# New due times and new groups for a list-scheduled kernel whose TensorE is nearly full

## The chip, the cores and the metric

One core of one Trainium2 chip. The time is device microseconds from the first to the last instruction, as the median of several executions. Nearly all executions of one kernel here lie within 1.5 us of its median, which is 0.3%; the worst is 2.4 us off. The kernel before took 531.44 us (530.61 to 532.65, three runs) when the prediction was made. A "look" below is one profiled execution of a kernel.

Ratios below are the mean time of one kernel's fast runs over the mean time of the other's in the same rounds on the same chip. They are not quite the ratio of the medians that are quoted beside them. The three sets of experiments ran on three chips, so ratios compare across sets and medians only roughly.

## The reference, cut to what matters

```python
# gated linear recurrence over 4 x 5824 tokens, 256 channels
a_t  = exp(8 * sigmoid(r) * log(a_base))
norm = sqrt(max(1 - a_t * a_t, 1e-6))
h    = a_t[:, t] * h + (norm * sigmoid(i) * x)[:, t]     # y[:, t] = h
# then a multiplicative feed-forward over the same 23296 tokens
out  = ((y @ w1) * (y @ w2)) @ w3 @ w_out                # 256 -> 1024 -> 1024 -> 256
```

The kernel multiplies `w3 @ w_out` once (the "fold", pieces `fold_t`, `fold_c`, `fold_m`, `fold_e`, eight of each), so that each token costs two up-projections and one down-projection. No run of this study does less.

## The kernel before: the parts that matter

The tokens are cut into 46 chunks. For each chunk, ScalarE computes tanh, decay and root, VectorE computes the gate, the scan and the product, GpSimd squares, multiplies and sometimes casts. TensorE takes the cast `y_t` through four pairs of up-projections and four down-projections:

```python
    def up(c, mp, nm, w_sb):
        pp = psum.tile([P, 2, CT], F32, name=nm, tag="pab")          # a ring of 3 for pa and pb
        for _ in range(warm.get((nm, c, mp), 0)):                      # warm-up matmuls
            nc.tensor.matmul(out=pp[:, 0, :P], lhsT=ident, rhs=ident, start=True, stop=True)
        ...                                                            # 4 matmuls of 512 columns

    def copy(c, mp):       # sa <- pa, PSUM to SBUF, on ScalarE (on VectorE if in DV_COPY): frees pa's buffer of the ring
    def product(c, mp):    # g_t <- sa * pb, on VectorE: frees pb's buffer of the ring
    def scan(c, cb):       # two of them for each chunk on VectorE, cut at a batch boundary
    def cast(c):           # y_t <- h_t, on VectorE or GpSimd
```

The ring explains most waits below. Where pairs follow each other, a `pa` takes the buffer of an earlier pair's `pb`, which the product frees. If that product stands behind a scan or a cast on VectorE, TensorE waits, although neither has anything to do with it.

The order of instructions isn't written down. A list scheduler runs inside the program that emits them: every job has a due time (a formula plus `OFFSET` by kind plus `SHIFT` by kind and chunk), each engine takes the ready job that is due first, and the result, sorted by start, is the order in which each engine's instructions are emitted. In that model, jobs of VectorE and GpSimd that carry a `lock` never overlap; its variable is called `port_free`, and "the port" below is this part of the model. What the chip does is told from the traces further down. Jobs whose `kind` needs another ScalarE table are batched by `group_sizes`; a table load took 1.28 us in the kernel before, each of its 31.

Of the kernel before, what the change touches and what calls it, by code (L numbers as in the profile page):

```python
# [20 lines left out]
def kernel(  # L21
# [28 lines left out]
    NCH = len(sizes)  # L50
    starts = [sum(sizes[:c]) for c in range(NCH)]

    group_sizes = [2, 1, 2, 3, 2, 2, 5, 4, 5, 2, 4, 4, 2, 2, 3, 3]
    assert sum(group_sizes) == NCH
    groups = []
    f = 0
    for n in group_sizes:
# [24 lines left out]
    T = {}  # L82

    N_LOG = 0
    TURN_R = {0, 1, 2, 3, 4, 5, 6, 8, 13}
    TURN_U = {0, 1, 2, 3, 5, 8, 9}
    DV_TIMES = {0, 1, 2, 8}
    DV_SQUARE = {2, 3, 10, 13}
    DV_CAST = {0, 2, 3, 7, 10, 11}
    DV_EVAC = set()  # L90
    DV_COPY = set()
    NHELD = 6
    NWF = 2
    FOLD_DMA = False
    FOLD_C, FOLD_E = "DVE", "DVE"
    W_CAST = {"w1": "POOL", "w2": "POOL", "wo": "POOL", "w3": "POOL"}
    BACKLOG = 1.05
    DUE_W, DUE_WH, DUE_W3, DUE_F = -45.0, 6.0, -22.0, 11.0
    LAG = 22.0
    D_LOAD, D_TANH, D_EXP, D_SQRT, D_GATE, D_SCAN, D_CAST = 66.0, -21.0, 2.0, 0.0, 11.5, 5.0, -14.0  # L100
    SPREAD = 4.4
    SLOT = 10.4
    M_OCC, M_LAT, M_PE = 0.04037856721, 0.02565538832, 0.0
    WARM = 80.0
    OFFSET = {"r": 8.5, "i": 8.0, "x": 6.0, "tanh_i": 3.5, "times": 3.0, "plus": -9.0, "turn_r": -12.0,
              "turn_u": -10.5, "decay": -1.5, "square": -2.0, "root": 6.5, "gated": 3.5, "scan": 0.5,
              "cast": -20.0, "copy": -1.0, "down": -3.5, "evac": -5.0, "store": -6.0}
    SHIFT = {("load", "w1"): -0.5, ("load", "w2"): 9.0, ("load", "wo"): 2.0, ("w1", 0): -27.0,
             ("w1", 1): -54.5, ("w2", 0): 2.5, ("w2", 1): -5.0, ("wo", 0): -1.0, ("wo", 1): -35.5,
             ("w3", 0): -64.5, ("w3", 1): 35.0, ("w3", 2): 4.5, ("w3", 3): 3.5, ("w3", 4): 13.0,  # L110
             ("w3", 5): 11.0, ("w3", 6): 23.5, ("w3", 7): 47.0, ("fold_t", 0): 9.5, ("fold_t", 1): -5.5,
             ("fold_t", 2): 4.0, ("fold_t", 3): 12.0, ("fold_t", 4): 2.0, ("fold_t", 5): 4.0,
             ("fold_t", 6): 1.5, ("fold_t", 7): -5.0, ("fold_c", 0): -5.5, ("fold_c", 2): 7.5,
             ("fold_c", 4): 2.5, ("fold_c", 5): 6.0, ("fold_c", 7): 11.5, ("fold_m", 0): -2.5,
             ("fold_m", 1): 2.5, ("fold_m", 2): -2.5, ("fold_m", 4): -5.5, ("fold_m", 5): 1.0,
             ("fold_m", 6): 9.5, ("fold_e", 0): 3.5, ("fold_e", 1): 2.0, ("fold_e", 2): 3.5,
             ("fold_e", 3): -4.0, ("fold_e", 4): 2.0, ("fold_e", 5): -4.5, ("fold_e", 6): 2.0,
             ("fold_e", 7): 2.0, ("r", 0): -16.0, ("r", 1): -13.0, ("r", 2): -5.5, ("r", 3): 3.5,
             ("r", 4): 3.0, ("r", 5): -6.0, ("r", 6): -0.5, ("r", 7): -6.5, ("r", 8): 0.5, ("i", 0): 1.0,
             ("i", 2): -2.0, ("i", 3): 2.0, ("i", 4): 4.0, ("i", 6): 3.5, ("i", 7): 4.0, ("i", 8): -1.5,  # L120
             ("x", 0): -2.5, ("x", 1): 1.0, ("x", 2): -1.0, ("x", 3): 1.5, ("x", 4): 5.0, ("x", 6): -4.0,
             ("x", 7): 4.5, ("tanh_r", 1): -2.5, ("tanh_r", 3): -2.0, ("tanh_r", 4): -0.5,
             ("tanh_r", 5): -1.0, ("tanh_r", 6): 2.0, ("tanh_r", 8): -3.5, ("tanh_i", 2): 4.0,
             ("tanh_i", 3): 8.0, ("tanh_i", 5): -7.5, ("tanh_i", 7): 9.0, ("tanh_i", 8): 2.0,
             ("times", 0): 3.5, ("times", 1): 2.0, ("times", 2): 5.0, ("times", 3): -8.5, ("times", 4): 5.0,
             ("times", 5): -2.0, ("times", 6): 1.0, ("times", 7): -1.0, ("times", 8): 6.0, ("plus", 0): -1.0,
             ("plus", 1): -4.0, ("plus", 2): 0.5, ("plus", 3): -1.5, ("plus", 4): 0.5, ("plus", 5): 19.5,
             ("plus", 6): 3.5, ("plus", 7): 1.5, ("plus", 8): -8.5, ("turn_r", 2): -1.0, ("turn_r", 3): 1.0,
             ("turn_r", 4): -1.0, ("turn_r", 5): -1.5, ("turn_r", 6): -4.0, ("turn_r", 8): 3.0,
             ("turn_u", 0): 1.5, ("turn_u", 1): -8.5, ("turn_u", 2): -18.0, ("turn_u", 4): 3.5,  # L130
             ("turn_u", 5): 9.5, ("turn_u", 6): -2.5, ("turn_u", 7): 3.5, ("turn_u", 8): 18.5,
             ("decay", 0): 2.5, ("decay", 1): 1.0, ("decay", 2): 5.5, ("decay", 3): -1.0, ("decay", 4): 3.0,
             ("decay", 5): 4.0, ("decay", 7): -2.5, ("decay", 8): -4.5, ("square", 1): -3.5,
             ("square", 2): 7.0, ("square", 3): -1.5, ("square", 4): 4.5, ("square", 5): -0.5,
             ("square", 6): -0.5, ("square", 8): -6.5, ("root", 0): 1.0, ("root", 1): 10.0, ("root", 2): 1.0,
             ("root", 5): -1.0, ("root", 6): -10.0, ("root", 7): 1.0, ("root", 8): 16.5, ("gated", 1): -4.5,
             ("gated", 2): -1.5, ("gated", 3): 5.0, ("gated", 5): -2.0, ("gated", 6): -3.5,
             ("gated", 7): -4.0, ("gated", 8): 1.0, ("scan", 0): 1.0, ("scan", 1): -11.5, ("scan", 2): 9.5,
             ("scan", 3): -2.0, ("scan", 4): -14.5, ("scan", 5): -6.5, ("scan", 6): 1.0, ("scan", 7): -1.0,
             ("cast", 0): 4.0, ("cast", 1): 2.0, ("cast", 3): 2.0, ("cast", 4): 1.0, ("cast", 5): -4.0,  # L140
             ("cast", 6): -1.5, ("cast", 7): -19.0, ("cast", 8): -4.0, ("pa", 1): 5.5, ("pa", 2): 23.0,
             ("pa", 3): 3.5, ("pa", 4): 2.0, ("pa", 5): -2.0, ("pa", 7): 1.0, ("pa", 8): 1.0,
             ("pb", 1): 12.5, ("pb", 2): -13.0, ("pb", 4): -0.5, ("pb", 5): 2.5, ("pb", 6): 2.5,
             ("pb", 7): -1.0, ("pb", 8): -2.0, ("copy", 0): 0.5, ("copy", 1): -1.0, ("copy", 2): 3.5,
             ("copy", 5): -2.0, ("copy", 6): -7.0, ("copy", 7): -2.0, ("product", 0): 4.5,
             ("product", 2): 2.5, ("product", 3): -2.5, ("product", 4): 0.5, ("product", 5): 2.0,
             ("product", 6): -5.0, ("product", 7): -2.5, ("product", 8): -2.0, ("down", 1): 4.5,
             ("down", 2): 3.0, ("down", 3): -2.5, ("down", 4): 12.5, ("down", 5): -1.0, ("down", 6): 3.0,
             ("down", 7): 4.0, ("down", 8): 0.5, ("evac", 2): 1.0, ("evac", 3): 1.0, ("evac", 4): 4.5,
             ("evac", 7): -6.0, ("store", 0): 8.5, ("store", 3): -3.0, ("store", 4): 3.0, ("store", 5): -4.0,  # L150
             ("store", 8): -2.0}
    src = {"r": rf, "i": jf, "x": xf}

    def flat(t):
# [7 lines left out]
    def long_rows(c):  # L162
        return c in TURN_R and c in TURN_U

# [14 lines left out]
    def tanh_r(c):  # L179
        n = sizes[c] // P  # L180
        t = gates.tile([P, NCB, 4, P], BF16, name="th_r", tag="th_r")
        if c in TURN_R:
            nc.scalar.activation(out=flat(t)[:, :n, :], in_=T["r", c][:, :n, :], func=AF.Tanh, scale=0.5)  # L183
# [129 lines left out]
    def copy(c, mp):  # L313
        w = sizes[c]
        sa = ffn.tile([P, 2, CT], BF16, name="sa", tag="sa")
        copy_to((c, mp) in DV_COPY, sa[:, :, :w], T["pa", c, mp][:, :, :w])
        T["sa", c, mp] = sa
# [20 lines left out]
    def evac(c, j2):  # L338
        T["ot", c, j2] = ffn.tile([P, 2, D], F32, name="ot", tag="ot")
        copy_to(c in DV_EVAC, T["ot", c, j2], T["po", c, j2])  # L340

# [131 lines left out]
    for k, g in enumerate(groups):  # L473
        log = k < N_LOG
        for c in g:
# [18 lines left out]
            for nm, key, tag, src_nm in (("turn_r", "pr", "rt", "thr"), ("turn_u", "pu", "ut", "u")):  # L494
                pre = ("tanh_r", c) if nm == "turn_r" else ("times", c, 1)
                d = V - D_TANH + 3.0 if nm == "turn_r" else U - D_GATE - 2.5
                if c in (TURN_R if nm == "turn_r" else TURN_U):
                    job((nm, c), "PE", 0.445 * f * (2 if c < 2 else 1), 0.445 * f * (2 if c < 2 else 1) + 0.22, d,
                        partial(turn_pe, c, key, src_nm),
                        [pre, ("ident",)] + [("turn_r", d) for d in g if nm == "turn_u" and d in TURN_R],  # L500
                        ("po", (key, c)), [(src_nm, c)])
# [37 lines left out]
            for j in range(sizes[c] // P):  # L539
# [11 lines left out]
                elif j % 2:  # L551
                    e, o, l = ("DVE", 0.599, 0.734) if c in DV_EVAC else ("ACT", 0.48, 0.63)
                    job(("evac", c, j // 2), e, o, l, t + 1.5, partial(evac, c, j // 2), [("down", c, j)],
# [18 lines left out]
    order = []  # L572
# [21 lines left out]
    while any(waiting.values()):  # L594
# [3 lines left out]
        for e in engines:  # L598
            if free[e] > t:
                continue  # L600
            key = next((k for k in waiting[e][:80] if startable(k, t)), None)
# [33 lines left out]

    nc.scalar.dma_start(out=la4, in_=a_param.rearrange("(cb p) -> p cb", p=P))

    table = None
    for _, _, key in sorted(order):
        kind = jobs[key]["kind"]  # L640
        if kind == 2 and table != 2:
            nc.scalar.preload_act_table_set("natural_log_exp_and_others")
        if kind is not None:
            table = kind
        jobs[key]["fn"]()
# [28 lines left out]
```

## Time and profile before

| what | value | read from |
|---|---|---|
| span of the profiled execution | 529.5 us | page |
| VectorE, ScalarE, GpSimd busy | 84, 87, 66% | page |

How TensorE's time divides into work and losses is worked out in the prediction below. I count TensorE's losses from start to start: the next matmul's start, less this one's start and its slot (0.056, 0.108 or 0.216 us for 128, 256 or 512 columns, after the spacing of starts at full clock: 0.056, 0.109 and 0.216 in the kernel before). Some matmul records are missing from most traces (3148 of 3204 are there in the first look at the changed kernel). One missing record of 512 columns looks like a loss of 0.216 and is left out; a real gap beside a missing record is too large by that much.

### The profile page before, as it was taken

To read this page: it belongs to the slowest core of one execution; us is meant where nothing else is said; L and a number is where in the kernel's file an instruction comes from. 1 tells how busy PE (TensorE), PEld (TensorE's weight loads), DVE (VectorE), ACT (ScalarE), POOL (GpSimd) and SP (SyncE) were. 2 spreads that over 40 slices of the span, in tenths; PEclk is the share of its full clock that TensorE was granted. 3 is DMA by queue.
4 is the path that set the end of the run, shared out by engine and by line. 5 is a ranking of instruction groups with operands and counts; after the bars stand their busy time and mean duration, and the time that the engine had idled before them with its cause. 6 is when DMAs were issued, how large, how long until landed. Compare 5 with 4: busy or idle time off the path is not lost.

```text
span 529.5 us, 8816 instructions
## 1 busy us (share of the span) xinstructions
PE 501.8 (95%) x3209; PEld 309.0 (58%) x3209; DVE 444.6 (84%) x373; ACT 459.2 (87%) x538; POOL 347.2 (66%) x270
## 2 busy tenths in 40 slices
PE   1299899999999999999999999999999999999997
PEld 1276576565655555666655565565666565665655
DVE  0798889998999988889797888898899799889642
ACT  6998698999899999989999999899999899884543
POOL 1579765569758883783878748968867677792000
PEclk9999899999999999999999999999999999999999
DMA  8999959889996998699898997969989898634112
GB/s 305 385 377 353 337 116 288 264 246 279 306 276 185 287 270 219 180 282 233 228 226 263 260 263 196 274 209 291 315 174 282 173 246 205 133 99 81 41 60 100
DMA packets 174604, 123.28 MB, mean 233 GB/s; under 512 B 84448, under 2 KB 170208, under 8 KB 174560
## 3 DMA queue, kind: packets, MB, share of 16 engines
q1 hardware_dynamic: 174288, 122.71, 85.0%
q8 instruction: 25, 0.41, 0.3%
q14 instruction: 19, 0.16, 0.1%
q10 hardware_dynamic: 272, 0.00, 0.0%
HBM read 78.91 MB, written 23.86 MB: 194 GB/s over the span
## 4 chain that ended last, share of the span: by engine, by line
PE 84%; ACT 6%; DVE 5%; issue 3%; DMA 2%; SPq 0%; DVEq 0%; ACTq 0%
PE pa L303 27%; PE pb L303 27%; PE po L334 27%; DVE g_t L323 3%; ACT sa L311 1%; PE pw L399 1%; DVE h_t L284 1%; DMA rt<-th_r 1%; ACT th_i L192 1%; ACT a_t L242 1%; DMA i_t<-in_i_gate_dram 1%; PE ptr L221 1%; ACT nrm L258 1%; DVE w3t L394 1%; ACT L192 0%
## 5 line engine op out<-in xcount | busy, mean ns | idle before, releaser
L323 DVE TENSOR_TENSOR g_t<-sa,pb 128x1024 bf16<-128x1024 bf16 (+1 forms) x184 | 219.1, 1198 | 55.5 <-ACT sa L311 47.3
L303 PEld LDWEIGHTS <-w_sb 128*128 128x128 bf16 x1472 | 144.1, 98 | 139.0 <-issue 5.0
L311 ACT CAST sa<-pa 128x1024 bf16<-128x1024 f32 (+1 forms) x184 | 183.5, 1000 | 37.5 <-PE pa L303 35.8
L303 PE MATMUL pa<-y_t,w_sb 128*128 128x512 bf16 (+1 forms) x736 | 188.3, 379 | 1.6 <-DVE g_t L323 1.3
L303 PE MATMUL pb<-y_t,w_sb 128*128 128x512 bf16 (+1 forms) x736 | 187.3, 377 | 0.6 <-DVE g_t L323 0.6
L334 PE MATMUL po<-wp_sb,g_t 128*128 128x256 bf16 x1456 | 184.5, 273 | 0.0
L334 PEld LDWEIGHTS <-g_t 128*128 128x128 bf16 x1456 | 142.4, 98 | 49.5
L284 DVE TENSOR_TENSOR_SCAN h_t<-a_t,h_t,nrm 128x512 f32<-128x512 f32 (+3 forms) x90 | 140.5, 1569 | 0.8
L249 POOL TENSOR_TENSOR nrm<-a_t 128x512 f32<-128x512 f32 (+1 forms) x84 | 107.9, 1300 | 20.9 <-ACT a_t L242 20.8
L213 POOL TENSOR_TENSOR u_t<-th_i,x_t 128x512 bf16<-128x512 f32 x78 | 116.2, 1508 | 0.5
L292 POOL CAST y_t<-h_t 128x1024 bf16<-128x1024 f32 x40 | 46.9, 1173 | 86.5 <-DVE h_t L284 72.9
L197 POOL TENSOR_SCALAR th_i<-th_i 128x1024 f32<-128x1024 f32 x42 | 53.2, 1268 | 20.6 <-ACT th_i L192 15.3
L311 ACT COPY ot<-po 128x512 f32<-128x512 f32 (+1 forms) x91 | 52.6, 580 | 15.8 <-PE po L334 14.6
L242 ACT ACTIVATE a_t<-rt,la 128x512 f32<-128x512 bf16 x74 | 58.8, 816 | 7.0 <-DMA rt<-th_r 6.1
L269 DVE SCALAR_TENSOR_TENSOR nrm<-nrm,ut 128x1024 f32<-128x1024 f32 x39 | 56.0, 1435 | 1.6 <-DMA ut<-u_t 1.6
L192 ACT ACTIVATE th_i<-i_t 128x1024 f32<-128x1024 f32 (+1 forms) x46 | 48.5, 1054 | 0.5 <-DMA i_t<-in_i_gate_dram 0.3
L258 ACT ACTIVATE nrm<-nrm 128x1024 f32<-128x1024 f32 (+1 forms) x46 | 47.6, 1053 | 0.2
L185 ACT ACTIVATE th_r<-r_t 128x1024 bf16<-128x1024 f32 x37 | 39.0, 1061 | 0.1
L221 PE MATMUL ptr<-ident,th_r 128*128 128x128 bf16 x68 | 6.8, 256 | 14.0 <-ACT th_r L183 14.0
L258 ACT ACT_TABLE_LOAD x14 | 18.0, 1283 | 0.2
L242 ACT ACTIVATE a_t<-ptr,la 128x512 f32<-128x512 bf16 (+1 forms) x18 | 12.6, 751 | 2.0 <-PE ptr L221 1.4
L221 PEld LDWEIGHTS <-th_r 128*128 128x128 bf16 x68 | 5.3, 115 | 15.3 <-ACT th_r L183 14.8
(39 smaller groups left out, 145.9 us busy)
## 6 DMA issues: line engine op xcount, KB each, us to landing
r_t<-in_r_gate_dram SPq DMA_DIRECT2D x45, 512.0 KB, 6.3
i_t<-in_i_gate_dram SPq DMA_DIRECT2D x45, 512.0 KB, 5.6
x_t<-in_x_dram SPq DMA_DIRECT2D x45, 512.0 KB, 4.9
out_dram<-ot SPq DMA_DIRECT2D x89, 256.0 KB, 3.6
wf<-in_moe_w_dram SPq DMA_DIRECT2D x12, 512.0 KB, 5.7
wf<-in_moe_w_out_dram SPq DMA_DIRECT2D x2, 512.0 KB, 6.4
ut<-u_t SPq DMA_TRANSPOSE x39, 4.5
rt<-th_r SPq DMA_TRANSPOSE x37, 4.7
```

Of the source, the lines that this page charges most:

```text
L192: nc.scalar.activation(out=t[:, :n, :], in_=T["i", c][:, :n, :], func=AF.Tanh, scale=0.5)
L197: nc.gpsimd.tensor_scalar(t, t, 1.0, 1.0, op0=ALU.add, op1=ALU.mult)
L213: nc.gpsimd.tensor_mul(out=u.rearrange("p cb j q -> p j cb q")[:, js], in0=cut(t)[:, js], in1=cut(T["x", c])[:, js])
L242: nc.scalar.activation(out=a, in_=pr, func=AF.Exp, scale=la4[:, cb:cb + 1], bias=la4[:, cb:cb + 1])
L249: eng.tensor_mul(out=T["n", c][:, cb, :w], in0=T["a", c][:, cb, :w], in1=T["a", c][:, cb, :w])
L258: nc.scalar.activation(out=T["n", c][:, :, :w], in_=T["n", c][:, :, :w], func=AF.Sqrt, scale=-1.0, bias=1.0)
L269: nc.vector.scalar_tensor_tensor(out=T["n", c][:, :, :w], in0=T["n", c][:, :, :w], scalar=1e-3, in1=T["pu", c][:, :, :w], op0=ALU.max, op1 ...
L284: nc.vector.tensor_tensor_scan(T["h", c][:, cb, lo:hi], T["a", c][:, cb, lo:hi], T["n", c][:, cb, lo:hi], init, ALU.mult, ALU.add)
L303: nc.tensor.matmul(out=pp[:, q, :w], lhsT=w_sb[:, cb, m * P:(m + 1) * P], rhs=T["y", c][:, cb, :w], start=(cb == 0), stop=(cb == NCB - 1))
L311: nc.scalar.copy(out=dst, in_=src_ps)
L323: nc.vector.tensor_mul(out=T["g", c][:, 2 * mp:2 * mp + 2, :w], in0=T["sa", c, mp][:, :, :w], in1=T["pb", c, mp][:, :, :w])
L334: nc.tensor.matmul(out=po, lhsT=T["g", c][:, k, j * P:(j + 1) * P], rhs=wp_sb[:, k, :], start=(k == 0), stop=(k == KD - 1), skip_group_che ...
```

## The change

It means to find a better order: due times, offsets, shifts and group sizes come from a longer search, in which the scheduler's model was replayed with the port taken in turns. The diff alters constants; a long one, cut to its core:

```diff
-    group_sizes = [2, 1, 2, 3, 2, 2, 5, 4, 5, 2, 4, 4, 2, 2, 3, 3]
+    group_sizes = [2, 1, 2, 3, 2, 2, 5, 4, 5, 3, 4, 2, 4, 2, 2, 3]
-    TURN_R = {0, 1, 2, 3, 4, 5, 6, 8, 13}
+    TURN_R = {0, 1, 2, 3, 4, 5, 7, 8, 13}
-    DV_EVAC = set()
-    DV_COPY = set()
+    DV_EVAC = {9}
+    DV_COPY = {(0, 1)}
-    DUE_W, DUE_WH, DUE_W3, DUE_F = -45.0, 6.0, -22.0, 11.0
+    DUE_W, DUE_WH, DUE_W3, DUE_F = -43.5, 8.0, -18.5, 12.0
-    D_LOAD, D_TANH, D_EXP, D_SQRT, D_GATE, D_SCAN, D_CAST = 66.0, -21.0, 2.0, 0.0, 11.5, 5.0, -14.0
+    D_LOAD, D_TANH, D_EXP, D_SQRT, D_GATE, D_SCAN, D_CAST = 73.5, -20.0, 4.0, -1.5, 24.0, 7.5, 19.0
...   (LAG, SPREAD, SLOT, M_OCC, M_LAT, all of OFFSET and SHIFT)
+    MOVES = []
+    plan = [key for _, _, key in sorted(order)]
+    places = {p for p, _ in MOVES}
+    rest = [key for p, key in enumerate(plan) if p not in places]
+    for p, to in MOVES:
+        rest.insert(to, plan[p])
-    for _, _, key in sorted(order):
+    for key in rest:
```

> **What bounds the kernel now.** I read the page first (shares of the span, slices), then the chain of waits, then TensorE's timeline with what ended its idle time, then windows around its gaps.
>
> ```profile
> PE 501.8 (95%) x3209; PEld 309.0 (58%) x3209; DVE 444.6 (84%) x373; ACT 459.2 (87%) x538; POOL 347.2 (66%) x270
> ...
> PE   1299899999999999999999999999999999999997
> ...
> PE 84%; ACT 6%; DVE 5%; issue 3%; DMA 2%; SPq 0%; DVEq 0%; ACTq 0%
> ```
>
> TensorE is full from the third slice on, and the chain that ended last is TensorE for 84% of the span. Its busy share counts pipelined spans, so I count issue slots instead, from start to next start. The chain shows 0.86 to 0.87 us for four 512-column matmuls (pa, pb), 0.87 for eight 256-column ones (po, pw), 0.45 for eight 128-column ones (ptr, ptw). The work is then: 360 pa/pb groups x 0.865 = 311.4, eight half-width ones x 0.435 = 3.5, 182 po groups x 0.868 = 158.0, 8 pw x 0.87 = 7.0, 8 ptw x 0.45 = 3.6, 15 ptr x 0.45 = 6.8, and 33 warm-up matmuls x 0.056 = 1.8: 492 us of a span of 529.5. So 37.5 us are lost. Where:
>
> ```profile
> 0.00:26.50 26.50, 6.11 (x48) 4.83 (x49) 11.27 (x16) 21.30 (x25) 10.28 (x14) 1.00 0.95 345
> ...
> 60.00:65.00 5.00, 4.66 (x36) 3.18 (x34) 3.82 (x4) 2.65 (x4) 4.68 (x4) 0.66 1.10 348
> ...
> 150.00:160.00 10.00, 8.66 (x53) 4.95 (x51) 9.93 (x9) 9.25 (x11) 2.54 (x2) 1.00 1.00 302
> 160.00:410.00 250.00, 250.00 (x1542) 150.67 (x1541) 221.44 (x175) 237.05 (x278) 187.36 (x142) 1.00 0.94 244
> ...
> 420.00:519.00 99.00, 99.00 (x607) 59.20 (x606) 79.28 (x63) 71.50 (x83) 48.58 (x36) 1.00 0.53 124
> ```
>
> The columns are the stretch, then busy time (and count) of TensorE, its weight load, VectorE, ScalarE, GpSimd, then clock, DMA share and GB/s. Before 26.5 us only 48 small transposes run (48 x 0.056 = 2.7 us): 23.8 us lost to filling the pipe. From 160 to 410 and from 420 to 519 TensorE has no gap at all. The rest is in few places:
>
> ```profile
> 26.50 1.80 PE L299 MATMUL pa<-ident 128*128 128x128 bf16 x15
> 28.10 1.06 PE L303 MATMUL pa<-y_t,w_sb 128*128 128x256 bf16 x4
> ...
> 36.83 1.02 PE L303 MATMUL pa<-y_t,w_sb 128*128 128x512 bf16 x4 [0.49 <-DVE g_t L323]
> ...
> 59.35 0.61 PE L385 MATMUL ptw<-ident,w_t 128*128 128x128 bf16 x8 [1.54 <-DVE wp_sb L416]
> ...
> 158.97 1.02 PE L303 MATMUL pa<-y_t,w_sb 128*128 128x512 bf16 x4 [0.81 <-DVE g_t L323]
> ...
> 519.19 7.15 PE L334 MATMUL po<-wp_sb,g_t 128*128 128x256 bf16 x64
> ```
>
> By starts: about 0.8 us lost near 36; 1.7 + 0.5 at 57 to 60; about 1.7 to the clock in 60 to 65 (5.0 us at 0.66: 5.0 x 0.34); about 1.0 at 99 to 107; about 1.8 at 153 to 159; 0.4 in scattered places. Together 8 us after the pipe is full. Another 1.9 us go to half clock between 26.5 and 30.3 (the 15 warm-up matmuls stand 0.107 us apart, not 0.056), and the tail after the last matmul's start at 526.1 is 3.4. Every wait names VectorE, most of them the product g_t that frees the PSUM pair which the next up-projection needs.
>
> [...] the busy sum of 501.8 includes overlaps, the slots sum to 492. [...] the stall at 57 to 60 is followed by a clock of 0.66 in 60 to 65. [...] a 128x512 scan takes 1.28 us when alone, 1.58 on the mean of 84, and the one at 99.58 took 2.35 as GpSimd multiplied. [...]
>
> **The change part by part.** It alters only the constants of a list scheduler that fixes the order of instructions on each engine; the launch runs the same arithmetic. MOVES is empty, so the new reordering code does nothing.
>
> - Counts. Transposes on TensorE stay 15 groups (chunk 7 in place of 6), transposes by DMA 76, table loads 31 (16 groups of chunks before and after, so no 2 x 1.28 us are saved), all matmuls but five warm-ups: 5 x 0.107 at half clock = 0.5 us. Total work of TensorE: 491.8 instead of 492.1.
> - Moved work: one 128x512 copy (chunk 0) and two 128x512 evictions of chunk 9 go from ScalarE to VectorE. ScalarE loses 0.59 + 2 x 0.58 = 1.8 us, VectorE gains about the same, an estimate from ScalarE's durations. On totals of 459 and 445 that is nothing; only the place counts.
> - Start. The comparison of orders shows the same first sixteen ScalarE instructions and the same VectorE sequence of gate, scan and cast for the first chunks; the load of x for chunk 0 moves ahead of r, i of chunk 0 stays the fourth load, and it is i that the chain waits for (5.19 us from 2.12). So the cast of chunk 0 still ends near 27.0. But in the kernel before, TensorE still had warm-ups queued until 28.1: 1.06 us behind that cast. With 10 of them the first pa starts near 26.5 + 10 x 0.107 = 27.6. Saved: 0.5 us, if VectorE lets it through; its copy for chunk 0 (about 0.6) fits in the 0.63 + 0.61 us it idled at 30 to 33.
> - 57 to 60 us. Both orders have the same VectorE run there (two scans, fold eviction, fold copy, two products, fold eviction, fold copy) and nine warm-ups behind it. The stall of 2.2 us should stay. The half clock of 1.7 us may or may not follow it[...]: expected change 0, spread 1.7.
> - 99 to 107 us. Before: scan, product, scan, cast, two products. After: product, two scans, cast, two products, so 2 x 1.28 + 0.7 us in one piece instead of about 2.0. I put +0.3.
> - 153 to 159 us. The chunk across the batch boundary keeps its pattern (two scans, product, two scans, cast, two products). Behind it one product now comes after the gate alone, not after gate and scan (-1.2), but an eviction of 0.6 is put before it: -0.6 of the 1.8.
> - The rest, 160 to 519, where nothing is lost now, is reordered wholesale (groups 3, 4, 2, 4, 2, 2, 3 for 2, 4, 4, 2, 2, 3, 3). I counted, for each chunk, TensorE slots between the product after which VectorE scans it and its first up-projection. The least lead was 6.1 us before, without a stall; it is 6.9 after. Summing VectorE's work between products against TensorE's slots shows one new tight place, chunk 40, +0.4.
> - Tail: the last 64 matmuls, evictions and stores stand in the same order: 0.
>
> Sum: -0.5 + 0 + 0.3 - 0.6 + 0.4 = -0.4 from what can be counted. A longer search ought to have found something that these counts don't show, so I add -1.0 for it, an estimate: a part of the 8 us. 531.4 - 1.4 = 530.0 us.
>
> **The rivals.** (a) The search removes most VectorE stalls (36, 99, 153 and the half clock: 0.8 + 1.0 + 1.8 + 1.7 = 5.3): 526 us. For it: its title says that the port[...] is now modelled. Against: the order around 36, 57 and 99 hardly changed. (b) The new order collides somewhere in 160 to 519, where there is now no loss to win back, since a scan of 2.35 us in place of 1.28 at a tight product costs about 1 us: three to five such places give 533 to 536. For it: VectorE is 88% busy there (221.44 of 250) and ScalarE 95%. Against: leads of 6.9 us or more. (c) A DMA transpose or load comes late[...]; ScalarE waited 6.1 us in all for rt already. It would show as an idle ScalarE, and cost 1 to 3 us.
>
> **Range and chances.** Most lost time is in the start (23.8) and the tail, which keep their order. A gain over 2% needs 10.6 us: all 8 us of stalls and more of the start than the warm-ups give. A loss over 2% needs some ten new stalls of 1 us. So within 2% is nearly sure: 0.955, faster 0.015, slower 0.03. Predicted 530.0 us, eight in ten between 527.0 and 533.5.
>
> **What would show it right or wrong.** Right: first pa at about 27.6; a gap again near 57 to 60 ended by the fold eviction; a smaller gap near 158; TensorE at 3204 matmuls. Wrong: first pa earlier than 27 or later than 28.5; no idle at 57; gaps past 160 that add up to over 3 us; a second stretch of half clock; waits of TensorE for a cast y_t, which would mean that a chunk came late, not a buffer.

The cuts marked in the recorded texts, here and below, take out passages on the hardware that no trace or run of this case shows. No term of the sum is among them: it came to -0.4 from what was counted and -1.0 on top, from 531.4 to 530.0. That the half clock may or may not follow the stall, with a spread of 1.7 (5.0 x 0.34), stands as the author's estimate.

## The result, and the profile after

| kernel | median us | range, runs | ratio to before, 95% interval |
|---|---|---|---|
| before, same rounds | 531.83 | 530.61 to 532.65, 4 | |
| changed | 530.65 | 530.53 to 531.21, 4 | 0.9982 [0.996, 1.0004] |
| changed, run again in set one | 530.74 | 529.49 to 531.87, 6 | 0.9974 [0.9958, 0.999] |

The change is worth 1.0 to 1.4 us, a quarter of a per cent; the interval of the first ratio still holds 1, that of the second, with more runs, doesn't. The page of the changed kernel, the lines that answer to those of before:

```profile
PE 497.2 (94%) x3148; PEld 308.3 (58%) x3204; DVE 442.2 (84%) x376; ACT 457.7 (86%) x535; POOL 341.3 (64%) x270
...
PE   1299899999999999999999999999999999999997
...
PE 79%; DMA 8%; DVE 5%; ACT 3%; issue 3%; POOL 1%; SPq 1%; DVEq 0%; ACTq 0%; POOLq 0%
```

The weight loads count 3204, so five warm-ups fewer than the 3209 of before, as planned; that only 3148 matmuls stand beside them is missing records. A TensorE that is "busy" 4.6 us less is no gain either: it is mostly those records. The windows of the changed kernel (stretch, then busy time and count of TensorE, weight load, VectorE, ScalarE, GpSimd, then granted clock, DMA share, GB/s):

```profile
60.00:65.00 5.00, 4.04 (x46) 3.21 (x47) 4.30 (x7) 3.68 (x5) 5.00 (x5) 1.00 1.08 363
...
150.00:160.00 10.00, 9.08 (x58) 5.48 (x57) 9.96 (x10) 9.33 (x10) 1.54 (x2) 1.00 1.02 298
160.00:410.00 250.00, 247.60 (x1503) 149.60 (x1530) 219.71 (x173) 234.95 (x278) 188.59 (x143) 1.00 0.96 247
```

The stretch from 60 to 65 ran at full clock (0.66 before). The stretch from 150 to 160 lost less. In 160 to 410, which was full before, some losses appeared. TensorE's timeline of the changed kernel shows the places (start, duration, instruction, and in brackets the idle time and what ended it):

```profile
26.33 1.04 PE L221 MATMUL ptr<-ident,th_r 128*128 128x128 bf16 x8 [3.41 <-ACT th_r L183]
27.16 1.27 PE L299 MATMUL pa<-ident 128*128 128x128 bf16 x10
28.23 1.06 PE L303 MATMUL pa<-y_t,w_sb 128*128 128x256 bf16 x4
...
60.56 0.61 PE L385 MATMUL ptw<-ident,w_t 128*128 128x128 bf16 x8 [1.43 <-POOL nrm L249]
...
61.95 1.05 PE L399 MATMUL pw<-wo_sb,w3t 128*128 128x256 bf16 x8 [0.34 <-DVE w3t L394]
...
153.27 0.81 PE L303 MATMUL pa<-y_t,w_sb 128*128 128x512 bf16 x3 [0.86 <-DVE g_t L323]
```

The wait at 60.56 is put down to GpSimd, whose square ended in the same instant; the fold eviction on VectorE that ended it before runs from 60.09 to 60.51 here too. By starts, in us lost, before against changed, of the two profiled executions:

| place | before | changed | predicted change |
|---|---|---|---|
| first up-projection starts at | 28.10 | 28.23 | -0.5 |
| wait for the folds, 57 to 62 | 1.71 + 0.50 | 1.59 + 0.50 | 0 |
| half clock after it | 1.7 | 0 | 0, spread 1.7 |
| full clock first granted at | 30.27 | 32.22 | none named |
| 99 to 107 | 0.96 | 0.84 | +0.3 |
| 152 to 158 | 1.83 | 1.03 | -0.6 |
| 160 to 520 | 0.4 | 1.76 (255: 0.36, 388: 0.84, 465: 0.56) | +0.4 |
| after the last matmul's start | 3.4 | 3.4 | 0 |

The spans of these two executions are 529.5 and 529.4, nearly equal. One pair of profiles can't explain a difference of 1.2 us in the medians, since each execution differs by as much from the next. So the experiments take several looks at the same order and time each kernel in five rounds.

**Where the start went.** ScalarE's first tanh, in the kernel before, then in the changed one:

```profile
4.14 0.63 ACT L183 ACTIVATE th_r<-r_t 128x512 bf16<-128x512 f32 x1 [1.65 <-DMA r_t<-in_r_gate_dram]
```

```profile
5.47 0.63 ACT L183 ACTIVATE th_r<-r_t 128x512 bf16<-128x512 f32 x1 [2.98 <-DMA r_t<-in_r_gate_dram]
```

The x load now stands ahead of r, and r lands 1.3 us later. That alone costs nothing, as ScalarE waits again behind this tanh. What counts comes next: first in the kernel before, then in the changed one:

```profile
7.34 0.63 ACT L192 ACTIVATE th_i<-i_t 128x512 f32<-128x512 f32 x1 [0.27 <-DMA i_t<-in_i_gate_dram]
```

```profile
7.05 1.06 ACT L183 ACTIVATE th_r<-r_t 128x1024 bf16<-128x1024 f32 x1 [0.95 <-DMA r_t<-in_r_gate_dram]
8.01 0.61 ACT L192 ACTIVATE th_i<-i_t 128x512 f32<-128x512 f32 x1
```

In the kernel before, ScalarE waits for i of chunk 0. In the changed one i has landed at 7.69, but ScalarE is still at the tanh of chunk 1's r until 8.1, whose load is now the third and not the second. In all fourteen looks of this study the first decay starts 2.91 us after i has landed where r is loaded first (seven looks), and 3.19 to 3.22 us after it where x is (seven). So the order of the loads costs 0.3 us. The rest of the 0.66 us by which the decay starts later (10.88 against 10.22) is i itself, which landed 0.38 later. Two looks at the kernel before differ by as much (7.31 and 7.71), so this can be chance. From the first decay to the first up-projection it is 17.88 us with 15 warm-ups and 17.33 to 17.36 with 10, in every look; so the five warm-ups are worth 0.53 us there, as predicted.

The cast of chunk 0 ends at 26.90 instead of 27.04, because two scans happened to run in 1.27 us instead of 2.06, but the transposes that TensorE does just ahead of its warm-ups come at 26.33 instead of 25.67. The warm-ups stand behind those in TensorE's order, so they begin at 27.16 and not at 26.5.

**Where the stall at 152 comes from.** VectorE in the kernel before:

```profile
147.98 2.24 DVE L284 TENSOR_TENSOR_SCAN h_t<-a_t,h_t,nrm 128x448 f32<-128x448 f32 x1
150.14 1.29 DVE L284 TENSOR_TENSOR_SCAN h_t<-a_t,nrm 128x64 f32<-128x64 f32 x1
151.47 1.62 DVE L292 CAST y_t<-h_t 128x1024 bf16<-128x1024 f32 x1
153.01 2.34 DVE L323 TENSOR_TENSOR g_t<-sa,pb 128x1024 bf16<-128x1024 bf16 x2
```

VectorE, then GpSimd, in the changed kernel:

```profile
149.16 1.29 DVE L284 TENSOR_TENSOR_SCAN h_t<-a_t,nrm 128x64 f32<-128x64 f32 x1
150.49 1.60 DVE L292 CAST y_t<-h_t 128x1024 bf16<-128x1024 f32 x1
152.01 2.34 DVE L323 TENSOR_TENSOR g_t<-sa,pb 128x1024 bf16<-128x1024 bf16 x2
154.27 0.68 DVE L309 COPY ot<-po 128x512 f32<-128x512 f32 x1
```

```profile
148.95 2.59 POOL L213 TENSOR_TENSOR u_t<-th_i,x_t 128x512 bf16<-128x512 f32 x2 [0.65 <-DMA ut<-u_t]
```

The order is the same in both: scan, scan of 64 columns, cast, then two products, the first of which TensorE waits for. The small scan takes 1.29 us and the cast 1.60 beside GpSimd's multiply. The added eviction (`ot`) stands behind both products, so it isn't in this wait at all; it stands ahead of a third product, for which TensorE doesn't wait.

### The profile page after: what moved, and what is told of

It reads as the page before. It is cut to its first block, busy times and chain, and to the rows that moved or that the text cites. A ratio compares the mean times of both kernels' runs of the same rounds, so it can differ in the third digit from the quotient of the medians.

```text
span 529.4 us, 8756 instructions
## 1 busy us (share of the span) xinstructions
PE 497.2 (94%) x3148; PEld 308.3 (58%) x3204; DVE 442.2 (84%) x376; ACT 457.7 (86%) x535; POOL 341.3 (64%) x270
## 4 chain that ended last, share of the span: by engine, by line
PE 79%; DMA 8%; DVE 5%; ACT 3%; issue 3%; POOL 1%; SPq 1%; DVEq 0%; ACTq 0%; POOLq 0%
PE po L334 27%; PE pa L303 25%; PE pb L303 25%; DMA wf<-in_moe_w_dram 3%; DVE g_t L323 2%; DMA r_t<-in_r_gate_dram 2%; DVE h_t L284 2%; DMA out_dram<-ot 1%; DMA wf<-in_moe_w_out_dram 1%; ACT sa L311 1%; ACT th_i L192 1%; ACT a_t L242 1%; POOL wo_sb L371 0%; ACT th_r L183 0%; POOL w_t L371 0%
## 5 line engine op out<-in xcount | busy, mean ns | idle before, releaser
L303 PE MATMUL pa<-y_t,w_sb 128*128 128x512 bf16 (+1 forms) x698 | 184.3, 378 | 3.9 <-DVE g_t L323 2.1
L334 PE MATMUL po<-wp_sb,g_t 128*128 128x256 bf16 x1456 | 181.0, 273 | 0.2
L284 DVE TENSOR_TENSOR_SCAN h_t<-a_t,h_t,nrm 128x512 f32<-128x512 f32 (+3 forms) x90 | 135.0, 1512 | 0.8
L213 POOL TENSOR_TENSOR u_t<-th_i,x_t 128x512 bf16<-128x512 f32 x78 | 117.9, 1528 | 1.0 <-DMA ut<-u_t 0.7
L249 POOL TENSOR_TENSOR nrm<-a_t 128x512 f32<-128x512 f32 (+1 forms) x84 | 98.6, 1188 | 14.7 <-ACT a_t L242 13.6
L292 POOL CAST y_t<-h_t 128x1024 bf16<-128x1024 f32 x40 | 50.1, 1252 | 89.5 <-DVE h_t L284 78.1
```

The costliest lines, as they stand in the source:

```text
L213: nc.gpsimd.tensor_mul(out=u.rearrange("p cb j q -> p j cb q")[:, js], in0=cut(t)[:, js], in1=cut(T["x", c])[:, js])
L249: eng.tensor_mul(out=T["n", c][:, cb, :w], in0=T["a", c][:, cb, :w], in1=T["a", c][:, cb, :w])
L284: nc.vector.tensor_tensor_scan(T["h", c][:, cb, lo:hi], T["a", c][:, cb, lo:hi], T["n", c][:, cb, lo:hi], init, ALU.mult, ALU.add)
L303: nc.tensor.matmul(out=pp[:, q, :w], lhsT=w_sb[:, cb, m * P:(m + 1) * P], rhs=T["y", c][:, cb, :w], start=(cb == 0), stop=(cb == NCB - 1))
L334: nc.tensor.matmul(out=po, lhsT=T["g", c][:, k, j * P:(j + 1) * P], rhs=wp_sb[:, k, :], start=(k == 0), stop=(k == KD - 1), skip_group_che ...
```

## The experiments

Theory: the time past 68 us is set by a handful of places where a product stands behind a scan, a cast or a gate on VectorE; the change moved these about and won little; whether such a place costs 0 or 1.3 us is decided by whether a GpSimd instruction runs beside the scan or the cast. The start was lost to x ahead of r. Rivals: the folds' wait at 58 us decides; or the eviction; or the half clock. All kernels gave correct results. Twelve ran, in three sets; the kernel before took 531.91, 531.75 and 531.61 us (11 runs each) in these.

In the edits, `put(key, ahead_of)` takes one job out of the finished order and puts it ahead of another; what each engine does otherwise stays as planned. `("product", 5, 2)` is the product of chunk 5 and pair 2, both counted from 0.

### Set one: the start and the wait for the folds

**The changed kernel again** (no edit).

> The changed kernel unaltered, a control. My theory: its gain of 0.2% is real but small (0.998, interval below 1.000 with five rounds), and a second trace shows the same gaps of TensorE: about 2.1 us at 59 to 62, 0.8 at 103 to 107, 1.0 at 152, 0.8 at 388, 0.6 at 465. Rival: the profiled pair differed only[...] (before had a second half-clock stretch of 3.4 us, after had none); then the ratio comes out at 1.000, and a second trace of the changed kernel can show a half-clock stretch after its gap at 59.

530.74 us, ratio 0.9974, as expected of an unchanged kernel. Its profile tells what belongs to the order and what to chance. The wait at 58 us is there again (2.09 us in all), the gap at 465 as well (0.56). The gap at 152 is 0.38 instead of 1.03, the one at 388 is gone, and three between 407 and 411 have come (1.19 together). And this look had a half clock, in the window from 60 to 65:

```profile
60.00:65.00 5.00, 4.44 (x36) 3.29 (x36) 3.53 (x4) 2.50 (x3) 5.00 (x5) 0.66 1.08 364
```

So its absence in the first look wasn't the change's doing.

**The changed kernel with chunk 0's x load back behind r.**

```diff
+    put(("x", 0), ahead_of=("i", 0))
```

> The changed kernel with one move: the load of x for chunk 0 goes back behind the two loads of r, as before the change. Theory: putting x first is what made r land late (first tanh at 5.47 instead of 4.14 us) and moved ScalarE's start chain by 0.66 us; with it back the first decay starts at 10.2 instead of 10.9, the transposes ahead of the warm-ups at 25.7 instead of 26.3, and the first up-projection at about 27.6 instead of 28.2. Time: 0.3 to 0.6 us less than the changed kernel if that start carries through. Rival: the next stages are held by VectorE, so the earlier start is lost by 60 us and the time is the same within 0.2 us.

531.09 us (529.12 to 531.8), ratio 0.998 [0.9961, 0.9998]. In the profile the first tanh is back at 4.27 and the first up-projection starts at 27.70, 0.5 us earlier. Of that, 0.3 is the order of the loads (see above), the rest the landing of i. The time is no shorter. The lead is gone at 60 us: the gaps ahead of the folds are longer (0.56 + 0.16 at 55, then the 1.71 + 0.50), and the seventh fold transpose starts at 60.0; the two looks at the changed kernel have 60.56 and 59.84. In this look, what was gained at the start is given back to the folds' wait.

**The kernel before with 10 warm-ups.**

```diff
+    warm["pa", 0, 0] = 10
```

> The kernel before with 10 warm-up matmuls ahead of the first up-projection instead of 15, nothing else. The prediction's step: each costs 0.107 us at half clock and they hold the first up-projection, so it starts at about 27.6 instead of 28.1 us. Theory A: time 0.5 us less (ratio 0.999). Theory B: the earlier start is absorbed by the wait for VectorE's product near 36 us, which comes no earlier, or the clock is granted later for it: ratio 1.000.

530.72 us (529.9 to 533.11), ratio 0.9981 [0.9962, 1.0001]. Its TensorE timeline:

```profile
26.57 1.27 PE L299 MATMUL pa<-ident 128*128 128x128 bf16 x10
27.64 1.06 PE L303 MATMUL pa<-y_t,w_sb 128*128 128x256 bf16 x4
...
55.40 0.62 PE L385 MATMUL ptw<-ident,w_t 128*128 128x128 bf16 x8 [0.92 <-POOL w_t L371]
...
59.98 0.61 PE L385 MATMUL ptw<-ident,w_t 128*128 128x128 bf16 x8 [1.54 <-DVE wp_sb L416]
```

The prediction's start, in its own words "26.5 + 10 x 0.107 = 27.6", is met where the loads are left alone. Again the lead doesn't last: a new wait for a weight cast of GpSimd (0.92) stands ahead of the sixth fold transpose, and the seventh starts at 59.98, against 59.35 and 59.8 in two looks at the kernel before. The interval of the ratio holds 1. But the ratio itself is as low as the changed kernel's 0.9982 and 0.9974, so these runs don't rule out that most of what the change gained is the five warm-ups fewer.

**The changed kernel with the gap at 59 to 62 filled.** Two pieces of up-projection were put into the fold's wait, with chunk 3's cast and one fold eviction moved ahead on VectorE so that they can start:

```diff
+    put(("cast", 3), ahead_of=("product", 2, 2))
+    put(("fold_e", 5), ahead_of=("product", 2, 3))
+    put(("pa", 3, 0), ahead_of=("fold_t", 6))
+    put(("pb", 3, 0), ahead_of=("fold_m", 6))
+    put(("copy", 3, 0), ahead_of=("decay", 8, 0))
+    warm["pa", 3, 0] = 0
```

> The changed kernel with the gap at 59 to 62 us filled: on VectorE the cast of chunk 3 goes ahead of the last two products of chunk 2 and a fold eviction between them; on TensorE the first up-projection pair of chunk 3 goes ahead of the seventh fold transpose, and the nine warm-ups there are dropped. Theory: the loss there falls from 2.1 to about 0.9 us, and as TensorE bounds the rest, about 1 us of the time goes (ratio to before 0.996). Rival: VectorE is the bound between 30 and 110 us, then the loss shows up again at the next tight product near 75 or 103 and the time stays within 0.3 us of the changed kernel.

531.22 us (530.12 to 532.96), ratio 0.9989 [0.9971, 1.0006]. TensorE loses 1.4 us instead of 2.1 at 57 to 62, and then this:

```profile
66.21 1.05 PE L399 MATMUL pw<-wo_sb,w3t 128*128 128x256 bf16 x8 [1.57 <-DVE w3t L394]
```

The last fold now waits for its VectorE copy, at 66. The rival holds in kind: VectorE binds there, not the order on TensorE. The copy runs from 65.48 on, behind a gate of 1.89 us that VectorE began at 63.66. Whether it is VectorE's amount of work or, again, its order that binds wasn't tested: neither this copy nor the fold eviction at 58 alone was moved ahead.

### Set two: the products

**The changed kernel with five products moved ahead on VectorE.**

```diff
+    put(("product", 5, 2), ahead_of=("cast", 7))
+    put(("product", 10, 1), ahead_of=("cast", 11))
+    put(("product", 20, 1), ahead_of=("gated", 22))
+    put(("product", 32, 3), ahead_of=("scan", 34, 0))
+    put(("product", 40, 1), ahead_of=("scan", 41, 1))
```

> The changed kernel with five VectorE products moved ahead of the casts, scans or gates that stood before them: those that TensorE waited for at about 103, 152, 255, 388 and 465 us (gaps of 0.8, 1.0, 0.36, 0.84 and 0.56 us in the first trace of it). Theory: each gap goes, as the product is what frees the PSUM pair, and the scan or cast has a lead of 6 us; so 1.5 to 2 us less than the changed kernel, a median of 528.8 to 529.3, ratio to before near 0.994. Rival: what VectorE does there in sum is what binds, so the gap moves to the next product or to the cast of the next chunk[...]: within 0.5 us of the changed kernel's 530.7.

529.14 us (528.19 to 530.49), ratio 0.9953 [0.9935, 0.9971]. The gap at 152 is 0.15, the ones at 255 and 465 are gone, 388 is 0.24; 0.60 at 106 and two of 0.3 are left. This is the lowest time of the study. It is below the kernel before; its interval overlaps that of the changed kernel (0.9958 to 0.999), but two later runs, with these five moves and one more, have 0.9963 and 0.9961. The mean of the three is 0.9959, that of the two runs of the changed kernel 0.9978.

**The changed kernel with the two evictions of chunk 9 on ScalarE again.**

```diff
+    DV_EVAC.clear()      # after the order is made, so the places stay
```

> The changed kernel with chunk 9's two evictions back on ScalarE, at the same places in the order. Theory: the gap near 152 us comes from the scans and the cast drawn out by GpSimd before the eviction, so without the eviction the gap stays between 0 and 1.3 us and the median is within 0.4 us of the changed kernel's 530.7. Rival, the term of the prediction: the eviction costs TensorE 0.6 us of the stall; then the gap is about 0.6 us smaller in the profile than the mean of the changed kernel's looks (1.03, 0.38, 0, 1.28) and the time 0.6 less.

531.44 us (529.62 to 533.72), ratio 0.9994 [0.9971, 1.0017]. The gap at 152 is 0.45, inside the range of the looks with the eviction (0, 0.38, 1.03, 1.28), and the time is not 0.6 lower. With the traces, in which TensorE never waits behind that eviction, the rival falls. The median is 0.7 higher than expected, with an interval that holds the changed kernel's ratio; I take nothing from that.

**The kernel before, a second look** (no edit).

> The kernel before, unaltered, a second profile of it. Theory: its gap near 153 to 159 us is caused by the order (two scans and a cast between two products) and shows again with 1.5 to 1.9 us; the gap of 1.7 + 0.5 near 58 shows again; the first grant of full clock falls anywhere between 28.5 and 32.5 us[...]. Rival: the gap near 153 is as much a matter of chance as the one of the changed kernel (0 to 1.3).

531.42 us, one run, its state unknown. The gap of 152 to 158 is there again with 1.80, and in the look with 10 warm-ups with 1.59: in the old order it came in all three looks. No half clock this time, so that is a matter of chance. And there is a gap of 1.05 at 316 that the first look hadn't: "no gap at all" from 160 on was true of one execution.

**The changed kernel with x back, the five products, and 18 small matmuls ahead of the seventh fold transpose.**

```diff
+    put(("x", 0), ahead_of=("i", 0))
+    (the five products as above)
+    def keep():
+        t = psum.tile([P, 2, CT], F32, name="pk", tag="pab")
+        for _ in range(18):
+            nc.tensor.matmul(out=t[:, 0, :P], lhsT=ident, rhs=ident, start=True, stop=True)
+    jobs["keep",] = dict(kind=None, fn=keep)
+    rest.insert(rest.index(("fold_t", 6)), ("keep",))
```

> The changed kernel with chunk 0's x load behind the r loads as before, the five products moved ahead as in the run with products, and 18 small matmuls into a free PSUM buffer ahead of the seventh fold transpose, to keep TensorE busy through the wait at 58 us. Theory: the gaps past 100 us go (-1.5 to -2) and no half clock follows the wait (-0.9 on the mean, as about half of the looks had one at 1.7), so a median of 528.0 to 529.0, 2 to 3 us below the kernel before, and no spread above 1.5 us. Rival: the moves give nothing, then 530 or more; or the small matmuls themselves delay the folds, up to +1.0.

531.1 us (530.46 to 533.29), ratio 0.999 [0.997, 1.0009]. A miss: three parts that each ought to help or do nothing lost what the products alone had won. The last set takes it apart.

### Set three: the parts of the miss, and the old order

**The five products and the small matmuls, without x.**

```diff
+    (the five products, and keep() as above)
```

> The changed kernel with the five products moved ahead, and the 18 small matmuls ahead of the seventh fold transpose, but x for chunk 0 left where the change put it. Theory: the small matmuls fill a wait that is there anyway, so the seventh transpose still starts near 60.5 us and the time is that of the run with products, 529.1, or up to 0.9 less, as no half clock follows; then it was x's place that spoilt the run with all three. Rival: the small matmuls hold a PSUM buffer or TensorE and cost 1 to 2 us, then 530.5 to 531.

531.22 us (529.98 to 533.31), ratio 0.9997 [0.9979, 1.0015]. So it is the small matmuls that cost some 2 us (0.9997 less 0.9953, of 531.7, is 2.3; with x back, 0.999 less 0.9963 is 1.4). They don't delay the fold they stand ahead of: the seventh transpose starts at 61.2, against 61.0 in the run with products alone, although this look began 0.8 us later (first up-projection at 29.12, as i landed at 8.57). In the profile the loss is far behind them, where ScalarE waits for a transposing DMA:

```profile
232.65 0.81 ACT L242 ACTIVATE a_t<-rt,la 128x512 f32<-128x512 bf16 x1 [2.26 <-DMA rt<-th_r]
233.37 0.56 ACT L311 COPY ot<-po 128x512 f32<-128x512 f32 x1
233.84 1.01 ACT L311 CAST sa<-pa 128x1024 bf16<-128x1024 f32 x1
```

In the run with products alone the same wait is 1.40, in the looks at the changed kernel's order 0.8 to 1.0. The copy `sa` stands behind it in order, its product behind that, and TensorE loses 0.5 us there and 0.25 to 0.7 at 241, 242 and 274. The look at the miss above has the same places with 1.2, 0.25, 0.4 and 0.76. This is of the kind of the prediction's rival (c). It isn't foreign to the original orders either: the gap of 1.05 at 316 in the second look at the kernel before stands behind a gate on VectorE that waited 1.30 us for another such DMA (`ut`). Why that DMA comes late at 230 with 18 matmuls at 60 us is open. Both looks fell on the slowest of their six executions, so they show the kind of loss rather than its mean size.

**The five products with x back.**

```diff
+    put(("x", 0), ahead_of=("i", 0))
+    (the five products as above)
```

> The changed kernel with the five products moved ahead and chunk 0's x load behind the r loads again. Theory: TensorE starts 0.5 us earlier, but the lead is lost by the wait for the folds at 58 us, as in the run with x alone[...], so the time is between 529 and 531. Rival: the earlier start adds to the products' gain, 528.5 or less.

529.7 us (528.83 to 530.91), ratio 0.9963 [0.9949, 0.9977]. x's place gives and takes nothing that can be seen beside 529.14; the products' gain stays. This look can't test what an earlier start is worth: i landed only at 8.09, and TensorE started at 28.34, as in the run with products alone (28.31).

**Six products.**

```diff
+    (the five products as above)
+    put(("product", 6, 0), ahead_of=("gated", 8))
```

> The changed kernel with six products moved ahead, the sixth the first product of chunk 6 ahead of chunk 8's gate (two VectorE instructions of 0.6 us that stood before it). In the profile of the run with five, TensorE lost 0.6 us there, at 106. Theory: that loss goes and the time is about 0.5 us below the run with five, 528.6. Rival: the loss passes to the up-projection behind, which waits for the product after it, or the later gate delays chunk 8; then 529 to 530.

529.49 us (528.56 to 531.03), ratio 0.9961 [0.9947, 0.9976]. The loss at 106 didn't go: it is 1.10 at 105 now. The time is in the rival's range, but the wait is one that neither theory named:

```profile
105.83 0.61 PE L221 MATMUL ptr<-ident,u_t 128*128 128x128 bf16 x8 [0.93 <-ACT ot L311]
```

A transpose on TensorE waits for ScalarE's eviction `ot` (105.19 to 105.78), which stands behind a tanh and a copy there, and VectorE then idles 0.40 us for that transpose.

**The kernel before with three of its own products moved ahead.**

```diff
+    put(("product", 5, 2), ahead_of=("cast", 7))
+    put(("product", 10, 1), ahead_of=("cast", 11))
+    put(("product", 10, 3), ahead_of=("scan", 12, 0))
```

> The kernel before with three of its own products moved ahead: of chunk 5 ahead of chunk 7's cast, two of chunk 10 ahead of chunk 11's cast and of chunk 12's first scan. Its gaps there are 0.3 to 0.6 us near 103 and 1.8 us at 152 to 158. Theory: what the changed kernel gained past 100 us can be had from the old order by these moves alone: the gap of 1.8 falls under 0.6, and the time is 1.3 to 1.8 us below the kernel before, ratio 0.997. Rival: the gap moves on, as VectorE has no slack there in the old order; ratio 0.999 or more.

530.12 us (528.67 to 530.69), ratio 0.9974 [0.9961, 0.9987]. VectorE there, in the same frame as the lines of before:

```profile
148.15 1.29 DVE L284 TENSOR_TENSOR_SCAN h_t<-a_t,nrm 128x64 f32<-128x64 f32 x1
149.37 1.19 DVE L323 TENSOR_TENSOR g_t<-sa,pb 128x1024 bf16<-128x1024 bf16 x1
150.48 0.68 DVE L292 CAST y_t<-h_t 128x1024 bf16<-128x1024 f32 x1
```

The small scan was drawn out to 1.29 again, as in the kernel before, and yet TensorE lost nothing from 150 to 160: the product no longer stands behind the cast. Three moves in the old order win as much as the whole search did.

### All looks beside each other

TensorE's losses past 68 us, summed from the profiles as told above (over 0.12 us):

| order | looks, us | mean |
|---|---|---|
| before (with 15, 15, 10 warm-ups) | 3.2, 5.0, 3.1 | 3.8 |
| before, three products moved | 1.7 | 1.7 |
| changed (twice, x back, gap filled, evictions back) | 3.6, 3.3, 2.1, 4.0, 3.1 | 3.2 |
| changed, products moved (five, with x back, six) | 1.6, 2.5, 2.0 | 2.1 |
| changed, products and small matmuls | 5.9, 5.1 | 5.5 |

Moving the products is worth 1.2 us by this count (3.23 - 2.05). By the clock it is the ratio 0.9953 less the mean of the changed kernel's two, 0.9978: 0.0025 of 531.7, or 1.3 us; with the mean of the three runs with products, 0.9959, it is 1.0. The two agree. For the changed kernel against the kernel before the count gives 0.5 us, the clock 1.0 to 1.4; the rest isn't located, and the five warm-ups fewer may be part of it (0.9981 in the run above).

The half clock came in two of the fourteen looks, in the kernel before and in the changed kernel's second. In the kernel before, the trace records it from 60.99 on, for 3.413 us; the 30.72 us of full clock ahead of it, from 30.27 on, are nine times that. So I laid pieces of 3.413 us from the first grant of full clock on, in every look, and summed TensorE's idle time in each one around 60 us. In the two looks with a half clock one piece held 2.21 and 2.09 us of idle time, and the half clock began at that piece's end, 60.99 and 61.49. In the other twelve no piece held more than 1.93. The wait is the same 2.1 to 2.2 us in most; whether one piece held all of it or two shared it differed with the first grant, which came anywhere from 28.6 to 32.2 us (at 32.22, in the first look at the changed kernel, two pieces held 0.76 and 1.55). That is what fourteen looks show, two half clocks among them; no run was made to test it.

## Why the prediction was right, and which steps were not

The number was right: 530.0 predicted, 530.65 measured, inside the range, and the same within 2%. That it came this close is partly luck: what could be counted summed to -0.4, and the rest of the -1.4 was a guess. The measured change is 1.0 to 1.4 us. By its own steps:

- **The bound, and the tail.** Right. TensorE stayed nearly full from 28 us on, the tail stayed 3.4 us, and no run of the study gained more than the 8 us of stalls hold (the most is 2.5, 0.9953). That is what made the class safe.
- **The start, -0.5.** Wrong, it came out at +0.13. The step that failed is that "it is i that the chain waits for". The cast ended at 26.90 as said ("near 27.0"), but with x ahead of r ScalarE is still at the tanh of chunk 1's r when i has landed (+0.29), and i itself landed later in this look (+0.38, within what two looks at one order differ); both delay the transposes that TensorE runs ahead of the warm-ups. The term for the warm-ups was right: -0.53. The sum of the three is the +0.13. The term bought nothing in TensorE's timeline either: the runs made for it start at 27.70 and 27.64 and have the seventh fold transpose at 60.0 and 59.98. Looks at the same orders that start later have it at 59.84 to 60.56 and at 59.35 to 59.8.
- **57 to 60, 0 with a spread of 1.7.** Right: 1.59 + 0.50 for 1.71 + 0.50, and the half clock came in two of the fourteen looks.
- **99 to 107, +0.3.** Not seen: it changed by -0.1 (0.96 to 0.84), within what two looks at one order differ.
- **152 to 158, -0.6.** The sum was too small. The -1.2 for the product that follows the gate alone was right: the mean of five looks at the changed order is 0.6 us, of three at the old 1.7, so -1.1. The +0.6 for the eviction was wrong: TensorE doesn't wait for the product behind it. What the prediction didn't see is the spread of the changed order, 0 to 1.3.
- **Chunk 40, +0.4.** Right: 0.56 in all five looks at the changed order, none in the three of before, and gone when that product is moved ahead.
- **The search's -1.0.** Unsupported, as it was when written. Only 0.5 us past 68 us are seen. The new order has a larger gap at 255 (0.35 to 0.36 in all five looks, 0.14 in the three of before) and others near 388 or 410 in some looks, so rival (b) came true in small. Its claim that a longer search ought to have found something holds for the median; where, isn't shown.

What lies behind most terms is how long a scan or a cast on VectorE takes when GpSimd is at work, and that can be read from the traces. In all fourteen looks, the 22 casts of 128x1024 on VectorE that began while no GpSimd instruction ran took 0.68 to 0.70 us. Of the 48 others, the 45 that began with over 0.2 us of a GpSimd instruction still to run took 0.54 to 0.55 us more than that rest, up to 1.72 in all. The scans of 64 columns do the same: 0.26 us in the four cases without, the rest plus 0.13 to 0.15 in the 24 with. In the five looks at the changed order, the instructions ahead of the product at 152 took:

| look | scan of 64 columns | cast | gap of TensorE |
|---|---|---|---|
| gap at 59 filled | 1.29 | 1.61 | 1.28 |
| first | 1.29 | 1.60 | 1.03 |
| evictions on ScalarE | 0.26 | 1.68 | 0.45 |
| second | 0.26 | 1.72 | 0.37 |
| x back | 0.26 | 0.69 | 0 |

In the last of them GpSimd's multiply started behind both (VectorE, then GpSimd):

```profile
148.85 0.26 DVE L284 TENSOR_TENSOR_SCAN h_t<-a_t,nrm 128x64 f32<-128x64 f32 x1
149.15 0.69 DVE L292 CAST y_t<-h_t 128x1024 bf16<-128x1024 f32 x1
```

```profile
149.23 2.98 POOL L213 TENSOR_TENSOR u_t<-th_i,x_t 128x512 bf16<-128x512 f32 x2 [1.25 <-DMA ut<-u_t]
```

The plan, which has the same order here in all five looks, didn't decide this: the multiply waits for a buffer that a DMA frees, and starts 0.21 us ahead of the small scan in the first look (148.95 and 149.16), between scan and cast in the second (150.56; 150.36 and 150.65), and 0.08 behind the cast with x back (149.23 and 149.15). A fraction of a microsecond changed which of them ran first. A product put ahead of the scan or the cast made it indifferent, as the run of the kernel before with three moves shows (scan 1.29, no loss). Five moves by hand, read from the traces, won about as much again as the search.

## What to carry to other kernels

Where one engine is full, read its remaining gaps one by one and ask what stands between the released work and its releaser in the releasing engine's order; a few such moves were worth as much here as new weights for the whole schedule (0.9974 for three moves, 0.9982 and 0.9974 for the weights), though not each of them helped. Look at one order several times before giving a gap of 1 us a cause: the ones that stay belong to the order, the others needn't (at 152 they came and went with GpSimd's work beside the scan and the cast: 0.26 or 1.29 us, 0.69 or 1.6 to 1.7). A gain at the start counts only if no later wait, here that of the folds, takes it back. And before an order is blamed for a late start, subtract what the loads' landing times alone differ by.
